# An eighth step of seven products in the second layer of an attention and gated-layer kernel, with a new order of all its steps

## The chip, the core and the metric

The kernel runs on one core of a Trainium2 chip. The metric is the device time of one execution in microseconds (us). Five engines work on it, each with a queue of its own that it takes strictly in order: TensorE (PE; its weight loads have a row of their own, PEld), VectorE (DVE), ScalarE (ACT), GpSimd (POOL) and SyncE (SP), which here issues almost all DMAs.

## What is computed

The reference is windowed attention with a few global keys, and a gated two-layer network on its result. Cut to what matters:

```python
# q, k, v: 4 batches, 8 heads, 768 positions, 64 per head; n_global = 8, n_local = 96
scores = matmul(q, k.T) / 8 + bias          # bias: -slope of the head * distance
keep = (pos_k < 8) | ((0 <= rel) & (rel < 96))
a = softmax(where(keep, scores, -1e9))
x = matmul(a, v)                            # 3072 tokens x 512
h = x @ w_in                                # 512 -> 2048
g = h * tanh(softplus(h))
out = g @ w_out                             # 2048 -> 512, float32
```

The two weights arrive as 64-bit floats and are turned into float32 on the chip. Products in full precision are made of three float16 products each: a number is split into a high half and a low rest, and high·high, high·low and low·high are summed.

## The kernel before

The 3072 tokens are cut into 12 chunks of 256 (two blocks of 128). Attention is done chunk by chunk in eight tiles t (a block and a pair of heads). The hidden layer is cut into eight steps of 256 hidden units. Step m = 8·chunk + fp stands for one step fp (0 to 7) of one chunk.

The order is written out by hand: `PROGRAM` (line 830) is a list of short commands, each a letter and a number. A loop at line 1036 calls the function of each, in a mode in which each engine gets its instructions in just that order. A mark ' behind a command gives its work to another engine. The commands that the prediction speaks of:

- `q`, `v`, `w`: loads of queries and keys, of values, of pieces of the weights. `A` to `E` turn a piece of the weights (0 to 31) into its halves.
- `s` (scores, PE), `t` (largest, DVE), `y` (exponentials, ACT), `g` and `p` (high half and rest of a tile, into a tile `hl` of a ring of three buffers), `X` (transposing DMA, frees the buffer), `W` (weighted sum of values, PE), `R`, `T`, `U`, `V` (rows of x, its halves, the transposing DMA). x's halves have a tile `xhl` of their own, in a ring of two.
- `i` (line 583): the first layer's product of a step, 24 matmuls of 256 columns into one of two `ph` banks. `j u n r` are four passes on ACT, `H` (line 607) the product that makes g and frees the bank.
- `z`, `Z`: high half and rest of g (tile `gt`). `o` (line 708) is the second layer's product of the step; it adds to the chunk's output in PSUM.
- `O` (line 397): a matmul of 512 columns on zeros, whose result nobody reads; there are 16.
- `k` (line 782): checks of ranges, whose last result `done_i` decides at the very end whether a slower program is to run.

A plain step `o` makes 12 matmuls of 512 columns: two token blocks, two hidden blocks, three half products (13 where one is cut in two). A fast step (`fast`, line 609) sees its two token blocks, two hidden blocks and two halves of the output's columns as a product of matrices of 2 by 2 blocks, and makes seven products of quarter blocks instead of eight: 7·3 matmuls of 256 columns. For that `J` (line 613) makes sums of g's blocks, so that `z` and `Z` work on 896 columns instead of 512, and `P`, `G`, `e`, `m` (lines 637 to 688) make, once for a step fp, the sums of w_out's quarters and their halves. Each of the seven products goes to one half of one of four PSUM banks: banks 0 and 1 are the output's, 2 and 3 hold what several quarters share. The corner `I` (line 732) reads banks 2 and 3 into a tile in SBUF, and the evacuation `Q` (line 743) adds that to banks 0 and 1. The list `FAST` (line 130) says from which chunk on a step fp is fast: 3 for fp 0 to 6, never for fp 7. So of each chunk from 3 on, seven steps are fast, and the eighth is plain: it writes banks 0 and 1 only, and banks 2 and 3 are through a step earlier.

```python
    FAST = (3,) * 7 + (NC,)
    PRODUCTS = ((0, 0, 2, 0), (2, 2, 0, 0), (6, 3, 0, 1), (1, 5, 1, 0), (3, 1, 3, 1), (5, 6, 2, 1), (4, 4, 3, 0))
```

An entry of `PRODUCTS` is the block of g, the block of weights, the bank and the half of the bank.

Of the kernel before, what the change touches and what calls it, by code (L numbers as in the profile page):

```python
# [108 lines left out]
def windowed(st, tc, loc):  # L109
# [20 lines left out]
    FAST = (3,) * 7 + (NC,)  # L130
# [642 lines left out]
    NX = 4 * NC  # L773
# [8 lines left out]
    def checks(i):  # L782
        if i == 0:
            nc.vector.tensor_scalar(ind[:, 0:2 * NC - 2], osum[:, 0:2 * NC - 2], 0.0, 0.0, op0=ALU.mult, op1=ALU.is_equal)
            nc.vector.tensor_scalar(ind[:, 2 * NC - 2:NX - 2], xmax, 1.0, None, op0=ALU.is_ge)
# [48 lines left out]
        s14 D1' S3' U1 y13 E1 O10 y12 g13' p10 W11 g12' t15 t14 A3' B3 C3 y14 S6' v2 D3' O12 A6 W10 p13 B6' C5 E2 s16 p12' t17 h2' y15 g14 w10 t16 p14 l2 y17 C6
        A10 y16 w8 w7 A8' O2 i0 B10 j0 g15' q5 g17 E3 D6' u0 p17' O13 s18 t18 x2 W13 S8 t19 W12 n0 w9 W14 p15 r0 y18 W15 w11 y19 D5 X17 E6 g16' O0 R2 V2 H0 B7
        s20 i1 g19 p16 z0' R3 t21 Z0 w12 T2 U2 p19 B8' y21 E5 X19 C8 V3 o0 t20 T3' U3 D8 j1 w14 S10' B9 u1 y20 A7 g21' i8 S7' h102 n1 C10 E8 C7 D7 s22 A9' p21'
        g20 l102 t23 j8 r1 X16 u8 H1 y23 p20 W17 X21 t22 n8 D10 B12 E7 X20 B11 w13 S11' z1' r8 i9 H8 w16 A12 g23' S12 Z1' W21 p23' y22 W16 A11 C12 E10 j9 A14'
        g22' g18 D12' X23 p22' u9 i2 C11 j2 n9 D11 X22 W19 p18' S14' r9 W20 S9' z8 B14' E11 u2 o1 H9 R4 C14 Z8 D14' E12' W23 i10 n2 r2 E14 X18 W22 w17 w18 T4 H2
        U4 w24 j10 u10 C9 W18 z2 n10 R5 z9 w20 D9' i3 Z2 Z9' o8 w15 r10 w19 w22 H10 j3 S18 A18' E9 S13' B16' q10 i11 S16' B18 A16 u3 S17' A17 C16 z10' A13' n3
        q7 C18 D16 B13' E16 o9 j11 C13 Z10' B17' C17 u11 D18 A20 E18' A15' r3 n11 D17 D13' E17 H3 E13' r11 B22' H11 w26 B20' S22' B15 A22' S24' v3 q6 z11 S20  # L840
        o10 i12 j12 z3' A19 u12 S15' C15 C22 i4 A24 D15' E15' w23 C20 Z3' w21 n12 B19' Z11' D20' B24 q8 r12 w25 S19 H12 o2 D22' A26 j4 u4 o3 C19 n4 E20 z12 C24
        r4 h3 D24 E22' D19' S21 B26 H4 N0 c7' E19 A21 S26' i5 j5 Z12' u5 S23' w27 B23 i13 B21' n5 C21 o11 A23 o12 C26 r5 E24' d7' D26 C23 H5 j13 A25 A27' z4'
        a7' u13 E26 V4 b7 S25' n13 B25' r13 i6 Z4' s24 H13 w29 C25 D21 D23 E23' z5 w28 t25 j6 i14 z13 u6 t24 n6 B27 S27' C27 q11 Z5' E21 T5 U5 D25 j14 w30 y24
        s26 r6 B28' D27 o4 A28 S28' g24' Z13' t26 o5 H6 c8 C28 p24 y26 w31 u14 E25 n14 V5 S30' z6' E27' t27 A30 D28' B30 o13 E28' C30 y27 l3 a8 r14 Z6 H14 D30
        A29' A31 S31 z14 y25 o6 E30 B31' g26 i7 d8' X24 i15 b8 p26' B29 Z14 C31 j7 g27 u7 n7 s28 r7 j15 u15 n15 v4 p27' S29' r15 q9 h4' H7 g25' a9 C29 o14 X27
# [197 lines left out]
```

## Time and profile before

| | before |
|---|---|
| median of 3 runs | 595.21 us (594.56 to 596.01) |
| the profiled execution | 594.36 us |
| its span, first to last instruction | 592.5 us |
| PE busy in the span | 577.9 us (98%) |
| DVE, ACT, POOL busy | 489.3, 478.3, 261.3 us |
| TensorE's granted clock | 1.0 of full speed |

The time of an execution is its span and 1.9 us around it. An engine's row on a page gives a group of instructions by line, tile and shape, their number, their busy time and the mean of one; behind the bar stands the idle time of the engine just before them, and what ended it. Matmuls overlap in the pipeline, so the busy time of one is more than the time by which it moves the next: for PE the prediction takes the distance between two starts.

### The profile page before, as it was taken

To read this page: it belongs to the slowest core of one execution; us is meant where nothing else is said; L and a number is where in the kernel's file an instruction comes from. 1 tells how busy PE (TensorE), PEld (TensorE's weight loads), DVE (VectorE), ACT (ScalarE), POOL (GpSimd) and SP (SyncE) were. 2 spreads that over 40 slices of the span, in tenths; PEclk is the share of its full clock that TensorE was granted. 3 is DMA by queue.
4 is the path that set the end of the run, shared out by engine and by line. 5 is a ranking of instruction groups with operands and counts; after the bars stand their busy time and mean duration, and the time that the engine had idled before them with its cause. 6 is when DMAs were issued, how large, how long until landed. Compare 5 with 4: busy or idle time off the path is not lost.

```text
span 592.5 us, 14936 instructions
## 1 busy us (share of the span) xinstructions
PE 577.9 (98%) x5652; PEld 466.6 (79%) x5652; DVE 489.3 (83%) x1272; ACT 478.3 (81%) x1112; POOL 261.3 (44%) x259
## 2 busy tenths in 40 slices
PE   6999999999999999999999999999999999999996
PEld 4887866567667789788889788888888888888884
DVE  6999999998999999989888986687888876663665
ACT  6999999999898998896786697677888678765661
POOL 0145422236316876552443474555563433444251
PEclk9999999999999999999999999999999999999999
DMA  9999999562562448654753653554574414240001
GB/s 228 312 276 191 254 308 242 151 148 66 118 150 55 114 95 137 100 117 122 166 115 68 126 127 80 94 118 107 88 178 58 101 38 90 54 91 19 36 2 38
DMA packets 132972, 73.76 MB, mean 124 GB/s; under 512 B 102144, under 2 KB 122624, under 8 KB 132896
## 3 DMA queue, kind: packets, MB, share of 16 engines
q1 hardware_dynamic: 132608, 72.63, 54.6%
q8 instruction: 45, 0.74, 0.5%
q14 instruction: 31, 0.25, 0.1%
q10 hardware_dynamic: 288, 0.14, 0.1%
HBM read 38.62 MB, written 6.29 MB: 76 GB/s over the span
## 4 chain that ended last, share of the span: by engine, by line
PE 77%; DVE 7%; DMA 6%; ACT 4%; issue 2%; POOL 2%; SPq 1%; DVEq 0%; POOLq 0%; ACTq 0%
PE ph L583 35%; PE pav L717 13%; PE po L717 10%; PE po L726 6%; PE sc L434 4%; PE sc L522 3%; PE pav L726 3%; DMA AT<-hl 2%; DMA vc<-v 2%; DMA wts<-w_in 1%; PE pav L518 1%; DMA qr<-qT 1%; DVE gf L607 1%; DVE gt L157 1%; DVE hl L157 1%
## 5 line engine op out<-in xcount | busy, mean ns | idle before, releaser
L583 PE MATMUL ph<-xT,wts 128*128 128x256 f16 x2304 | 265.6, 273 | 2.7 <-DVE gf L607 2.5
L583 PEld LDWEIGHTS <-wts 128*128 128x128 f16 x2304 | 222.3, 98 | 35.4 <-issue 5.4
L717 PEld LDWEIGHTS <-gt 128*128 128x128 f16 x1323 | 127.7, 98 | 16.7 <-issue 2.0
L157 POOL TENSOR_TENSOR gt<-gf,gt 128x896 f16<-128x896 f32 (+1 forms) x40 | 72.0, 1803 | 71.5 <-DVE gt L151 48.3
L590 ACT ACTIVATE e<-ph 128x512 f32<-128x512 f32 x96 | 56.4, 588 | 58.3 <-PE ph L583 55.9
L457 ACT ACTIVATE A<-A,nm 128x232 f32<-128x232 f32 (+1 forms) x192 | 88.3, 462 | 17.5 <-DVE nm L448 17.3
L607 DVE SCALAR_TENSOR_TENSOR gf<-e,ph 128x512 f32<-128x512 f32 x96 | 65.5, 682 | 32.1 <-ACT e L602 19.1
L157 POOL TENSOR_TENSOR hl<-A,hl 128x512 f16<-128x512 f32 (+1 forms) x39 | 47.5, 1224 | 78.5 <-DVE hl L151 48.4
L448 DVE CUSTOM_DVE_ANT_0 A<-sc,mb 128x232 f32<-128x232 f32 (+1 forms) x192 | 63.4, 375 | 11.7 <-PE sc L434 6.7
L726 PEld LDWEIGHTS <-gt 128*128 128x128 f16 x405 | 38.5, 98 | 40.8 <-issue 0.4
L598 ACT ACTIVATE e<-e,part 128x512 f32<-128x512 f32 x96 | 68.8, 717 | 2.1
L594 ACT ACTIVATE e<-e,ones 128x512 f32<-128x512 f32 x96 | 68.8, 717 | 1.8
L726 PE MATMUL po<-wts,gt 128*128 128x512 f16 (+1 forms) x309 | 68.4, 373 | 0.0
L157 DVE TENSOR_TENSOR gt<-gf,gt 128x896 f16<-128x896 f32 (+1 forms) x56 | 60.3, 1079 | 8.2 <-ACT gt L153 7.6
L157 POOL TENSOR_TENSOR wts<-ws,wts 128x512 f16<-128x512 f32 x22 | 30.0, 1366 | 74.0 <-ACT wts L153 28.0
L717 PE MATMUL pav<-wts,gt 128*128 128x256 f16 x378 | 62.0, 273 | 0.0
L602 ACT ACTIVATE e<-e 128x512 f32<-128x512 f32 x96 | 59.9, 624 | 1.7
L717 PE MATMUL po<-wts,gt 128*128 128x256 f16 x378 | 51.6, 273 | 0.0
L617 POOL TENSOR_TENSOR gf<-gf 128x128 f32<-128x128 f32 x41 | 23.2, 566 | 54.1 <-DVE gf L607 52.3
L151 DVE TENSOR_SCALAR gt<-gf 128x896 f16<-128x896 f32 (+1 forms) x51 | 31.5, 619 | 15.3 <-POOL gf L619 8.8
L153 ACT ACTIVATE gt<-gf 128x896 f16<-128x896 f32 (+1 forms) x45 | 36.5, 812 | 7.2 <-POOL gf L619 3.4
L457 ACT ACTIVATION_READ_ACCUMULATOR A<-A,nm 128x1 f32 x192 | 36.2, 189 | 0.0
(173 smaller groups left out, 900.8 us busy)
## 6 DMA issues: line engine op xcount, KB each, us to landing
qr<-qT SPq DMA_DIRECT2D x24, 256.0 KB
wts<-w_in SPq DMA_DIRECT2D x12, 512.0 KB
wts<-w_out SPq DMA_DIRECT2D x12, 512.0 KB
kr<-kd SPq DMA_DIRECT2D x32, 184.0 KB
out<-wr SPq DMA_DIRECT2D x11, 512.0 KB
vr<-v SPq DMA_DIRECT2D x10, 512.0 KB
vc<-vo SPq DMA_DIRECT2D x15, 192.0 KB
wr<-w_in SPq DMA_DIRECT2D x4, 512.0 KB
```

The source lines that it names most:

```text
L153: nc.scalar.activation(out, in_, AF.Copy, scale=scale)
L157: (nc.vector if other else nc.gpsimd).tensor_tensor(out, in_, high, op=ALU.subtract)
L448: nc.vector.tensor_tensor_reduce(out=A[:, j, 0:w], in0=sc[j][:, 0:w], in1=m, scale=-1.0 / (UNIT if ci < CF32 else UNIT * SQ), scalar=3.0e3 ...
L457: nc.scalar.activation(A[:, j], A[:, j], AF.Exp, bias=nm[:, h:h + 1], scale=-1.0, accum_out=rs[:, h:h + 1])
L583: nc.tensor.matmul(ph[:, j, :].rearrange("p (b t) -> p b t", b=2), wv4[:, 2 * fb, x, c * P:(c + 1) * P], xT[:, :, y * NCC + c, :], start=( ...
L590: nc.scalar.activation(mish[m]["e"], mish[m]["h"], AF.Exp, scale=1.0 / (SV * SW), accum_out=esum[:, m:m + 1])
L594: nc.scalar.activation(e, e, AF.Square, bias=ones)
L598: nc.scalar.activation(e, e, AF.Ln, bias=part, scale=SV * SW / SG / 2.0)
L602: nc.scalar.activation(e, e, AF.Exp, scale=-1.0)
L607: nc.vector.scalar_tensor_tensor(gf, mish[m]["e"], SG / (SV * SW), mish[m]["h"], op0=ALU.subtract, op1=ALU.mult, accum_out=gsum[:, m:m + 1])
L717: nc.tensor.matmul(pos[ci][bank][:, side * HN:(side + 1) * HN], gt[:, x, i, :], w[y], start=not begun[ci][bank], stop=n == 2 and fp == NFP ...
L726: nc.tensor.matmul(pos[ci][bank][:, c], gt[:, x, 2 * j + 1 - bank, :], wv4[:, 2 * fb + 1, y, c], start=not begun[ci][bank], stop=last and ...
```

## The change

`FAST` has 3 for all eight steps, and `fast` leaves out step 95, the last of the last chunk. So the eighth steps 31, 39, 47, 55, 63, 71, 79 and 87 become fast; step 95 stays plain. The weight sums of fp 7 have 4 KB per partition of their own (`four`), with all four quarter sums in one tile. The products stand in another order: the four for banks 2 and 3 first, the three for banks 0 and 1 last. In chunks 3 to 10 nothing is added to the second half of bank 1 any more; the corner writes that quarter of the output itself, with its sum for the checks (`osum3`), and `Q` adds one quarter less. x's halves have no ring of their own: they share the ring `hl` of three buffers. The whole table `PROGRAM` is replaced by another order, and several commands are given to another engine. The eight new steps bring eight commands `J` (31, 39, ..., 87) and `P7`, `G7`, `e7`, `m7`; the rest of the commands, the 16 `O` among them, are the same.

```diff
-    FAST = (3,) * 7 + (NC,)
+    FAST = (3,) * 8
...
+    four = cp.tile([P, 2, 4, DM // 2], F16, name="four")
...
+    osum3 = cp.tile([P, NC], F32, name="osum3")
+    nc.gpsimd.memset(osum3, 0.0)
...
-        xhl = at.tile([P, 2, DM], F16, name="xhl")
+        xhl = at.tile([P, 2, 2, W], F16, name="hl", bufs=3).rearrange("p a b w -> p a (b w)")
...
-        return ci >= FAST[fp]
+        return ci >= FAST[fp] and m != NC * NFP - 1
+
+    def whole_chunk(ci):
+        return all(fast(ci * NFP + fp) for fp in range(NFP))
...
+        elif fp == NFP - 1:
+            return (four,)
...
+        if fp == NFP - 1:
+            return [(w, four)]
...
+        if fp == NFP - 1 and k in (1, 4, 5, 6):
+            return [four[:, y, max(k - 3, 0), :] for y in range(2)]
...
-    PRODUCTS = ((0, 0, 2, 0), (2, 2, 0, 0), (6, 3, 0, 1), (1, 5, 1, 0), (3, 1, 3, 1), (5, 6, 2, 1), (4, 4, 3, 0))
+    PRODUCTS = ((0, 0, 2, 0), (5, 6, 2, 1), (3, 1, 3, 1), (4, 4, 3, 0), (2, 2, 0, 0), (6, 3, 0, 1), (1, 5, 1, 0))
...
-            for i, k, bank, side in PRODUCTS:
+            ends = {2: 1, 3: 3} if fp == NFP - 2 and not whole_chunk(ci) else {2: 1, 3: 3, 0: 5, 1: 6} if last else {}
+            for q, (i, k, bank, side) in enumerate(PRODUCTS):
...
+        if whole_chunk(ci):
+            into, total = out_tile(ci)[:, 0, HN:], osum3[:, ci:ci + 1]
+            nc.vector.scalar_tensor_tensor(into, end[:, 1, :], BACK, c[:, 1, :], op0=ALU.mult, op1=ALU.add, accum_out=total)
+            return
...
-        J91 r93 H93 j92 u92 z91' n92 i94 J93' r92 j94 u94 Z91' H92 J92' o90 z92' Z92 n94 z93' r94 H94 i95 J94 o91 j95 Z93' o92 o93 z94' u95 n95 Z94 r95 H95 k1
-        z95 Z95' k3 o94 I11 o95 Q11 k2
...
+        F0 j93 u93 n93 Y10 J89' z89' Z90 Z89 H91 i92 r93 J91 j92 H93 z91' u92 i94 J93 n92 Z91 j94 r92 H92 o89 J92' z92' u94 o90 z93' n94 Z92' r94 o91 i95 j95
+        o92 H94 u95 J94' Z93' n95 z94' k0 Z94 o93 r95 H95 z95' o94 Z95 I11' k1 o95 Q11 k3 k2
```

What the new order moves is shown at three places. The first is the end of DVE's queue (L739 to L741 are the corner, L753 the evacuation of the last chunk, L803 and L804 the last two of ten small operations of the third check, L809 and L810 the last check). Before:

```order
L803 TENSOR_SCALAR v_125<-v_125 1x1
L804 SCALAR_TENSOR_TENSOR v_125<-v_125,fl 1x1
L739 TENSOR_TENSOR vr<-vr 128x256
L740 SCALAR_TENSOR_TENSOR vr<-pav_8820,vr 128x512
L741 SCALAR_TENSOR_TENSOR vr<-pav_8820,vr 128x256
L753 SCALAR_TENSOR_TENSOR wr,osum<-po_8817,vr 128x512
L753 SCALAR_TENSOR_TENSOR wr,osum<-po_8818,vr 128x512
L809 TENSOR_SCALAR last<-sc 1x2
L810 SCALAR_TENSOR_TENSOR done_i<-last,v_125 1x1
L73 TENSOR_LOAD done_i
```

After, from the second evacuation on (L776); the next row is the one that writes `done_i`:

```order
L776 SCALAR_TENSOR_TENSOR wr,osum<-po_8916,vr 128x512
L819 TENSOR_SCALAR v_126<-sc 1x58
L820 TENSOR_REDUCE v_128<-v_126 1x1
L821 TENSOR_SCALAR v_128<-sc 1x1
L822 TENSOR_TENSOR v_128<-v_128 1x1
L823 TENSOR_REDUCE v_127<-sc 1x12
L824 TENSOR_REDUCE v_128<-v_127 1x1
L825 TENSOR_REDUCE v_128<-sc 1x1
L826 TENSOR_TENSOR v_128<-v_128 1x1
L827 TENSOR_SCALAR v_128<-v_128 1x1
L828 SCALAR_TENSOR_TENSOR v_128<-v_128,fl 1x1
L833 TENSOR_SCALAR last<-sc 1x2
```

The ten operations of the third check stood ahead of the corner, and stand between the last evacuation and the last check.

The second place is PE's queue at the same end; L794 and L818 are the third check's product. Before, between steps 93 and 94:

```order
L717 LDWEIGHTS gt
L717 MATMUL pav_8820<-qr,gt 128x256
L794 MATMUL sc<-ind,ones 1x145
L717 LDWEIGHTS gt
L717 MATMUL pav_8819<-wts,gt 128x256
```

After, behind the last product of step 95 (L739):

```order
L739 LDWEIGHTS gt
L739 MATMUL po_8916<-wts,gt 128x512
L818 MATMUL sc<-ind,ones 1x157
L831 MATMUL sc<-osum,ones 1x2
L73 TENSOR_LOAD done_i
```

The check's product went from ahead of step 94 to behind step 95.

The third place is the start of SP's queue, behind the first load of queries and keys (vo and vc are values, wts the weights, 512 KB a piece). Before; the next row is the second load of vo:

```order
L335 DMA wts<-w_in 128x4x256
L175 DMA qr<-qT 128x2x256
L178 DMA kr<-kd 64x2x264 x2
L215 DMA vo<-v 128x2x512
L232 DMA vc<-v 96x512
L233 DMA vc<-v 8x512
L175 DMA qr<-qT 128x2x256
L178 DMA kr<-kd 64x2x368 x2
L335 DMA wts<-w_in 128x4x256 x2
L337 DMA wts<-w_out 128x1024 x2
L175 DMA qr<-qT 128x2x256
L178 DMA kr<-kd 64x2x368 x2
```

After, the same stretch:

```order
L336 DMA wts<-w_in 128x4x256 x2
L176 DMA qr<-qT 128x2x256
L179 DMA kr<-kd 64x2x264 x2
L216 DMA vo<-v 128x2x512
L233 DMA vc<-v 96x512
L234 DMA vc<-v 8x512
L176 DMA qr<-qT 128x2x256
L179 DMA kr<-kd 64x2x368 x2
L338 DMA wts<-w_out 128x1024
L336 DMA wts<-w_in 128x4x256
L176 DMA qr<-qT 128x2x256
L179 DMA kr<-kd 64x2x368 x2
```

One piece of the weights moved ahead of the second load of queries and of the first values; ahead of the second chunk's values there are four pieces instead of five.

## Rows read from the trace of the kernel before

**Rows 1.** The page: the span, PE's busy time, the granted clock in 40 slices, and the chain that ended last by engine.

```profile
span 592.5 us, 14936 instructions
PE 577.9 (98%) x5652; PEld 466.6 (79%) x5652; DVE 489.3 (83%) x1272; ACT 478.3 (81%) x1112; POOL 261.3 (44%) x259
...
PEclk9999999999999999999999999999999999999999
...
PE 77%; DVE 7%; DMA 6%; ACT 4%; issue 2%; POOL 2%; SPq 1%; DVEq 0%; POOLq 0%; ACTq 0%
```

**Rows 2.** Busy time by stretch of the span: the stretch, its length, then busy us and number of instructions of PE, PEld, DVE, ACT and POOL, the granted clock, the DMA engines' busy share and GB/s.

```profile
0.00:60.00 60.00, 52.91 (x415) 41.93 (x416) 53.29 (x201) 52.27 (x155) 18.91 (x24) 1.00 1.00 251
60.00:150.00 90.00, 88.82 (x728) 61.60 (x726) 85.43 (x197) 87.72 (x192) 34.12 (x27) 1.00 0.75 195
150.00:200.00 50.00, 49.14 (x481) 33.61 (x479) 47.62 (x105) 46.21 (x107) 22.47 (x21) 1.00 0.52 107
200.00:260.00 60.00, 59.93 (x655) 50.62 (x654) 56.83 (x146) 54.23 (x134) 41.13 (x41) 1.00 0.59 114
260.00:560.00 300.00, 299.52 (x3148) 255.84 (x3145) 226.36 (x577) 224.89 (x506) 134.51 (x141) 1.00 0.45 93
```

**Rows 3.** PE in order of time in chunk 4, start and length in us: a fast step `o` from 281.48 until the `i` step at 283.77, and the plain eighth step from 286.39 until the attention's products at 288.98.

```profile
281.48 0.49 PE L717 MATMUL pav<-wts,gt 128*128 128x256 f16 x3
...
283.44 0.49 PE L717 MATMUL pav<-ws,gt 128*128 128x256 f16 x3
283.77 2.78 PE L583 MATMUL ph<-xT,wts 128*128 128x256 f16 x24
286.39 2.75 PE L726 MATMUL po<-wts,gt 128*128 128x512 f16 x13
288.98 0.25 PE L522 MATMUL sc<-vc,AT 104*128 104x64 f16 x3
```

**Rows 4.** The view of the waits: engine and line, what it waited for, us in total, how many waits, the longest.

```profile
ACT hl L153 <- DMA AT<-hl: 3.6, 3, 2.0
...
DVE hl L151 <- DMA AT<-hl: 3.0, 2, 2.4
...
PE ph L583 <- DVE gf L607: 2.5, 3, 1.2
...
PE sc L522 <- DMA AT<-hl: 0.8, 2, 0.4
```

**Rows 5.** Groups by line with different shapes apart: us busy, mean ns of one, idle time before them. The `gt` rows on DVE and POOL are `Z` with 896 and with 512 columns, the `hl` row is `p` on DVE.

```profile
L717 PEld LDWEIGHTS <-gt 128*128 128x128 f16 x1323 | 127.7, 98 | 16.7 <-issue 2.0 <-ACT A L457 0.2
...
L594 ACT ACTIVATE e<-e,ones 128x512 f32<-128x512 f32 x96 | 68.8, 717 | 1.8
...
L607 DVE SCALAR_TENSOR_TENSOR gf<-e,ph 128x512 f32<-128x512 f32 x96 | 65.5, 682 | 32.1 <-ACT e L602 19.1 <-POOL gt L157 8.9 <-POOL gf L619 1.8
L602 ACT ACTIVATE e<-e 128x512 f32<-128x512 f32 x96 | 59.9, 624 | 1.7
L590 ACT ACTIVATE e<-ph 128x512 f32<-128x512 f32 x96 | 56.4, 588 | 58.3 <-PE ph L583 55.9 <-DVE gf L607 1.9
...
L157 DVE TENSOR_TENSOR gt<-gf,gt 128x896 f16<-128x896 f32 x36 | 43.4, 1204 | 4.9 <-ACT gt L153 4.4
...
L157 DVE TENSOR_TENSOR hl<-A,hl 128x512 f16<-128x512 f32 x37 | 28.7, 776 | 1.5 <-ACT hl L153 1.5
...
L157 POOL TENSOR_TENSOR gt<-gf,gt 128x512 f16<-128x512 f32 x13 | 15.9, 1227 | 7.5 <-ACT gt L153 4.9 <-DVE gt L151 1.4 <-DVE rs L529 1.2
...
L641 DVE TENSOR_TENSOR vr<-wts 128x1024 f32<-128x1024 f16 x6 | 7.6, 1265 | 0.1
```

**Rows 6.** The start: PE in order of time, with the idle time before an instruction in brackets (28.18 is the first product with the second chunk's windows of values; 31.94 an `O`, 32.17 what follows it).

```profile
28.18 0.41 PE L518 MATMUL pav<-vc,AT 104*128 104x64 f32 x2 [0.73 <-DMA vc<-v]
...
31.94 0.39 PE L401 MATMUL po<-AT 128*128 128x512 bf16 x1
32.17 0.60 PE L480 MATMUL ph<-ident,A 128*128 128x128 f32 x4
```

**Rows 7.** The end in order of time: the third check's product and operations, the corner's first reading, the last step, the second evacuation, and the last check.

```profile
582.03 0.41 PE L794 MATMUL sc<-ind,ones 128*1 128x145 f32 x2
582.37 0.50 PE L717 MATMUL pav<-wts,gt 128*128 128x256 f16 x3
582.48 0.20 DVE L795 TENSOR_SCALAR v<-sc 1x46 f32<-1x46 f32 x1 [1.23 <-PE sc L794]
...
583.96 0.21 DVE L804 SCALAR_TENSOR_TENSOR v<-v,fl 1x1 f32<-1x1 f32 x1
...
584.55 0.60 ACT L153 ACTIVATE vr<-pav 128x512 f32<-128x512 f32 x1 [4.02 <-PE pav L717]
584.68 2.76 PE L726 MATMUL po<-wts,gt 128*128 128x512 f16 x13
...
587.47 0.69 DVE L753 SCALAR_TENSOR_TENSOR wr<-po,vr 128x512 f32<-128x512 f32 x1
...
588.22 0.19 PE L807 MATMUL sc<-osum,ones 128*1 128x2 f32 x2 [0.79 <-DVE wr L753]
588.45 0.15 DVE L809 TENSOR_SCALAR last<-sc 1x2 f32<-1x2 f32 x1 [0.28 <-PE sc L807]
588.63 0.21 DVE L810 SCALAR_TENSOR_TENSOR done_i<-last,v 1x1 int32<-1x1 f32 x1
```

More of the change, by code (lines that the diff above doesn't have):

```diff
@@ L713, in moe_out @@
         if fast(m):
-            for i, k, bank, side in PRODUCTS:
+            ends = {2: 1, 3: 3} if fp == NFP - 2 and not whole_chunk(ci) else {2: 1, 3: 3, 0: 5, 1: 6} if last else {}
+            for q, (i, k, bank, side) in enumerate(PRODUCTS):
                 w = factor(fp, k)
                 for n, (x, y) in enumerate(((0, 0), (0, 1), (1, 0))):
-                    nc.tensor.matmul(pos[ci][bank][:, side * HN:(side + 1) * HN], gt[:, x, i, :], w[y], start=not begun[ci][bank], stop=n == 2 and fp == NFP - 2 and (i, k) in ((5, 6), (4, 4)))
+                    nc.tensor.matmul(pos[ci][bank][:, side * HN:(side + 1) * HN], gt[:, x, i, :], w[y], start=not begun[ci][bank], stop=n == 2 and ends.get(bank) == q)
                     begun[ci][bank] = True
@@ L740, in corner, with out_tile @@
         nc.vector.scalar_tensor_tensor(c[:, 1:3, :], end, BACK, c[:, 3:4, :].broadcast_to([P, 2, HN]), op0=ALU.mult, op1=ALU.add)
+        if whole_chunk(ci):
+            into, total = out_tile(ci)[:, 0, HN:], osum3[:, ci:ci + 1]
+            nc.vector.scalar_tensor_tensor(into, end[:, 1, :], BACK, c[:, 1, :], op0=ALU.mult, op1=ALU.add, accum_out=total)
+            return
         nc.vector.scalar_tensor_tensor(c[:, 3, :], end[:, 1, :], BACK, c[:, 1, :], op0=ALU.mult, op1=ALU.add)
+    def out_tile(ci):
+        obs[ci] = raws.tile([P, DM, 2], I32, name="wr", bufs=3).bitcast(F32).rearrange("p f w -> p (f w)").rearrange("p (t m) -> p t m", t=2)
+        return obs[ci]
     def evacuate(ci):
         po = pos.pop(ci)
-        obs[ci] = raws.tile([P, DM, 2], I32, name="wr", bufs=3).bitcast(F32).rearrange("p f w -> p (f w)").rearrange("p (t m) -> p t m", t=2)
+        if ci not in obs:
+            out_tile(ci)
         for bank in range(2):
@@ L752, in evacuate @@
                 c = corners[ci]
-                nc.vector.scalar_tensor_tensor(obs[ci][:, t].rearrange("p (b m) -> p b m", b=2), po[bank].rearrange("p (b m) -> p b m", b=2), BACK, c[:, bank:bank + 3:2, :], op0=ALU.mult, op1=ALU.add, accum_out=osum[:, n:n + 1])
+                k = 1 if bank and whole_chunk(ci) else 2
+                nc.vector.scalar_tensor_tensor(obs[ci][:, t].rearrange("p (b m) -> p b m", b=2)[:, 0:k], po[bank].rearrange("p (b m) -> p b m", b=2)[:, 0:k], BACK, c[:, bank:bank + 2 * k - 1:2, :], op0=ALU.mult, op1=ALU.add, accum_out=osum[:, n:n + 1])
             if ci == NC - 1:
@@ L770, in flags @@
         nc.vector.tensor_scalar(fl[:, 3:4], L.n_f[0:1, 1:2], float(NLMAX), fl[:, 2:3], op0=ALU.is_le, op1=ALU.mult)
-    NX = 4 * NC
+    NX = 5 * NC
     NG = NC * NFP
@@ L834, in windowed @@
[L834 to L845, printed above, removed]
@@ new lines, in windowed @@
+        u74 i76 n74 T20' j76 U20 x11 u76 r74 X87 J72 n76 W83 H74 J74 W87 o70 X86 r76 W86 d23 z72' V20 o71 R21 s88 I8' t88 Z72 T21 y88 H76 t89 i75 U21 j75 J76
+        i77 g88' y89 u75 s90 Q8 z76' n75 j77 g89 o72 r75 t91 Z76 H75 o73 p89 u77 n77 p88' y91 z74 J75' t90 i78 V21 g91 z75 r77 s92 Z74 p91' j78 H77 X88 X89 Z75
+        u78 t92 Y8 t93 J77 y92 o74 n78 r78 y93 g92' i79 H78 g93' s94 j79 p92' u79 J78' y90 i80 t95 n79 X92 y95 z77' g90' p93 r79 j80 u80 o75 t94 z78 W89 Z77'
+        n80 X93 p90 H79 W92 o76 r80 J79' Z78 i81 y94 j81 z79' u81 H80 J80 n81 X91 o77 g95' r81 Z79' i83 o78 j83 p95' z80' g94 H81 i84 o79 p94' W88 W93 X94 u83
```

97 lines of the change are left out of this document (53 added, 44 removed).

## The prediction

> **What bounds the kernel now.** I read the page first: PE is busy 577.9 of 592.5 us, the clock is full throughout, and PE has 77% of the chain that ended last [rows 1]. The reader is to see that no other engine is above 83%. The table by stretch then says where there is room beside PE [rows 2]. From 260 to 560 us PE is busy 299.52 of 300 us while DVE and ACT have about 75 us to spare; there PE alone sets the pace. From 60 to 200 us all three are full: DVE is busy 133 of 140 us, ACT 134. So a product taken from PE is worth its whole length after 260 us, and ahead of that as long as DVE and ACT keep up. Last I read what PE waits for: apart from start and end little, 2.5 us for DVE's product that frees a bank of the first layer, 0.8 us for transposing DMAs [rows 4], and 0.73 us for the second chunk's windows of values [rows 6]. What PE does not do any more therefore comes off the end, if its waits stay as they are.
>
> **The eight eighth steps.** A fast step takes PE from 281.48 to 283.77, 2.29 us, the plain eighth step from 286.39 to 288.98, 2.59 us [rows 3]. That is 109 ns for a matmul of 256 columns and 216 for one of 512. The eight steps that become fast give 8 × (2.59 − 2.29) = **2.4 us**, all of it on PE. Each fast step has nine more matmuls, and so nine more weight loads of 98 ns [rows 5]. In the fast step shown, 21 of them hide behind the matmuls, so I take nothing for them; the bound on the other side is a rival below. The Trainium skill, page "TensorE: Matmul & The Clock Gate", section "Back-to-back issue gap", speaks against this edit: it gives a stream of loads and matmuls a spacing of 81 ns at 128 columns and 131 at 512. My estimate from it is 98 ns at 256, so a fast step would take 2.05 us and a plain one 1.57, and the eight steps would lose 3.8 us. The trace disagrees, with 109 and 216 ns in the rows named.
>
> **What the fast steps add beside PE.** `J` for eight steps, 896 instead of 512 columns in `z` and `Z`, and once `P7`, `G7`, `e7`, `m7`. At least six of the eight new steps lie after 260 us, where DVE has 74 us to spare [rows 2]; that work I cost at nothing. Step 31 and the weight sums lie between 150 and 260 us, and to be safe I count step 39 there too. On DVE they add 1.27 for `P7`, 1.38 for `m7` (the 1204 ns of 896 columns, scaled to 1024) and 2 × 0.5 for `Z`'s 384 more columns (the same row, scaled), some 3.7 us [rows 5], where DVE has 2.38 + 3.17 = 5.55 us idle [rows 2]. It fits; if it did not, each us over would be a us of PE. `Q` loses a quarter and the corner gains nothing, so nothing there.
>
> **The corner comes later.** Before, banks 2 and 3 were through a whole step ahead; now they are through only in the eighth step. The products' new order softens that: bank 2 is done after two of seven products, bank 3 after four. The tightest places are steps 47 and 87, behind which only one `i` step (2.62 us by the start of what follows [rows 3]) stands before the next chunk writes the banks. From bank 2's last product to there PE has 5 × 0.33 + 2.62 = 4.3 us, and the corner's reading and evacuation need 0.60 and four passes on DVE of at most 0.69 us [rows 7], 3.4 in all. The next chunk, moreover, begins with banks 2 and 3. I take nothing, with an upper bound of 8 × 0.3 us.
>
> **The end.** This is the part in which the new order costs. Before, the third check's product (0.34 us of PE, 582.03 to 582.37) and its ten operations on DVE (582.48 to 584.17, 1.69 us) run beside step 94. Then the second evacuation ends at 588.16, and the last check writes `done_i` at 588.84, 0.68 us later, after which only the fixed ending follows [rows 7]. Now the ten operations stand behind the second evacuation, DVE takes its queue in order, and `done_i` needs them: 1.69 + 0.39 for the last check and some 0.05 between, 2.13 us instead of 0.68. PE is spared the 0.34 us. The sum is 1.45 − 0.34 = **+1.1 us**. Nothing makes it smaller, since the ten follow the same evacuation in the same queue. It could be 0.35 more, since the second check's operations now stand between corner and evacuation. `done_i` is what the rows end with, so the output's store does not hide it. Step 95 itself moves closer to its `i`: three fast steps, 6.9 us, stand between them instead of four. Four passes on ACT (2.65 us), the product (0.68), a high half (at most as much) and a rest on POOL (1.23) make 5.3 us [rows 5]. That still fits.
>
> **The start.** Three `O` fewer stand behind the third `s` (seven instead of ten); they went to where PE waits for the first loads. An `O` moves what follows by 0.23 us (31.94 to 32.17 [rows 6]), so this gives between 0.7 us and nothing, if PE then waits instead; I take −0.3. One piece of the weights less is ahead of the second chunk's values. 512 KB at 251 GB/s [rows 2] are 2 us, more than the wait of 0.73 us [rows 6]. But another piece went ahead of the second queries and first values, which come 2 us later. The bounds are −0.73 and +2; I take −0.5, nearer the end at which a wait is seen.
>
> **All other moves.** The order of several hundred commands is new, and for the waits that come and go in the middle I have no term. The waits that are there, 2.5 + 0.8 us [rows 4], bound the gain; the loss is bounded by the rivals. I take nothing.
>
> **The sum.** −2.4 + 1.1 − 0.3 − 0.5 = −2.1 us. The profiled execution of 594.36 us would be 592.3; the median of 595.21 is 0.85 us above it, so the forecast is **593.1 us**.
>
> **Rivals.**
>
> - *The shared ring eats it.* A ring of three buffers that served 80 attention tiles serves 20 halves of x too. ACT and DVE wait 3.6 + 3.0 us on its transposing DMAs now [rows 4]. A quarter more users would add 1.7 us, and these waits fall where both engines are full. For it: the order that freed the tiles is another one. Against it: PE is behind them by a step or more in most places. Then 593.1 + 1.7 = 594.8 us, no difference that can be told (a measurement here tells 0.2%, some 1.2 us).
> - *DVE becomes the bound between 150 and 260 us.* The order gives DVE eight more of `p`, at up to 0.78 us [rows 5]. If all fell into that stretch, DVE would have 3.7 + 6.2 = 9.9 us more to do where it has 5.55 idle. It decides from 5.55 us on; at the full 9.9 PE waits 4.3 us more, and the time is 597.4 us: slower. Against it: they have 592 us to fall into.
> - *The new order waits less.* If it also removes the 3.3 us of waits in the middle, the time is 589.8, and half of them 591.5.
> - *Weight loads set the pace.* If the nine more loads of a fast step were exposed, 9 × 98 ns, an eighth step would take 0.58 us more than before, and the time would be 593.1 + 2.4 + 4.7 = 600.2 us. The fast steps of rows 3 speak against it. The page named above would have it go that way, with its smaller numbers.
>
> That the change does not do what it says I leave out: the eighth step's products on the new tile stand in PE's queue.
>
> **How the numbers follow.** The forecast has 0.48, with its own range of 592 to 594.2; the ring 0.25; DVE 0.13; fewer waits 0.13; weight loads 0.01. Faster by over 0.2% (below 594.0) are fewer waits and nearly all of the forecast, 0.13 + 0.44 = 0.57. Within it are the ring but for 0.01, and the forecast's upper edge, 0.28. Slower (above 596.4) are DVE, the weight loads and that 0.01, 0.15. For 8 in 10 I leave out weight loads, most of DVE's 597.4 and the far end of fewer waits: 590.8 to 596.6 us.
>
> **What the profile will show.** If I am right: 21 matmuls of 256 columns in 2.29 us for steps 31 to 87; in the last us ten small operations on DVE between the second evacuation and the last check, and `done_i` some 2.1 us behind the evacuation; no idle time of PE for the second chunk's windows; PE's waits in the middle between 2 and 5 us. PE idle before `i` with DVE as the cause between 150 and 260 us would show DVE as the bound. ACT or DVE idle before `hl` for transposing DMAs by much over 6.6 us would show the ring. If the first loads make PE wait for queries or values, my start is wrong.

## The result, and the profile after

The changed kernel takes 599.97 us (599.08 to 600.79, 6 runs) beside 595.19 us for the kernel before (594.53 to 596.36, 6 runs). The ratio is 1.0078, with a 95% interval of 1.0062 to 1.0093: it is slower by 4.6 us. Run again beside the later experiments it gave 599.75 us and 1.0065 (1.0051 to 1.0080). The prediction was 593.1 us, with a range up to 596.6: wrong in size and sign.

The profiled execution took 600.36 us, its span 598.6. First the page, as [rows 1]:

```profile
span 598.6 us, 15159 instructions
...
PE 578.9 (97%) x5713; PEld 473.4 (79%) x5716; DVE 503.6 (84%) x1293; ACT 482.2 (81%) x1119; POOL 273.6 (46%) x271
...
PEclk9998999999999999999999999999999999999999
...
PE 39%; DVE 5%; ACT 2%; issue 2%; POOL 1%; DMA 1%; DVEq 0%; POOLq 0%
```

The last row adds up to half the span only: the chain was followed back no further, and its shares are not to be set beside those of before. PE is no less busy than before, though it has less to do; the half clock of the fourth slice is a part of that. DVE is busy 14.3 us more, POOL 12.3. Busy time by stretch, with the columns of [rows 2]:

```profile
0.00:60.00 60.00, 52.48 (x385) 40.67 (x389) 50.90 (x190) 48.89 (x143) 17.36 (x25) 0.97 1.01 243
60.00:150.00 90.00, 90.00 (x756) 61.80 (x755) 85.17 (x215) 88.23 (x194) 32.89 (x26) 1.00 0.76 194
150.00:200.00 50.00, 49.14 (x478) 35.12 (x477) 47.49 (x104) 47.32 (x110) 24.19 (x22) 1.00 0.56 125
200.00:260.00 60.00, 58.84 (x633) 49.49 (x632) 55.99 (x134) 53.99 (x132) 43.94 (x44) 1.00 0.51 110
260.00:360.00 100.00, 96.47 (x1040) 82.89 (x1038) 86.67 (x212) 79.81 (x189) 50.12 (x53) 1.00 0.56 118
360.00:560.00 200.00, 198.87 (x2144) 175.49 (x2142) 153.99 (x382) 148.21 (x326) 90.00 (x90) 1.00 0.38 80
```

The same view of the kernel before, for the stretch in which PE lost most:

```profile
260.00:360.00 100.00, 99.98 (x1055) 85.07 (x1052) 87.22 (x216) 75.95 (x179) 42.33 (x43) 1.00 0.55 117
```

From 260 to 360 us PE, which was idle for 0.02 us, now stands still for 3.5 us. DVE is no busier there than before (86.67 against 87.22 of 100 us). So no engine is full, and still PE waits.

The waits, as [rows 4]:

```profile
DVE hl L152 <- DMA AT<-hl: 4.1, 4, 1.6
PE ph L586 <- DVE gf L610: 3.9, 5, 2.1
...
ACT hl L154 <- DMA xT<-hl: 1.7, 1, 1.7
```

PE's wait for `H` (now L610), which frees a bank of the first layer, grew from 2.5 to 3.9 us. The waits for `hl` fell from 6.6 to 5.8 us.

A fast eighth step (step 55) on PE in order of time, as [rows 3]:

```profile
383.27 0.49 PE L730 MATMUL pav<-wts,gt 128*128 128x256 f16 x3
383.60 1.15 PE L730 MATMUL pav<-four,gt 128*128 128x256 f16 x9
384.58 0.82 PE L730 MATMUL po<-wts,gt 128*128 128x256 f16 x6
385.23 0.49 PE L730 MATMUL po<-four,gt 128*128 128x256 f16 x3
385.56 1.69 PE L586 MATMUL ph<-xT,wts 128*128 128x256 f16 x14
```

It takes 2.29 us, as predicted.

PE's first large waits, with the idle time in brackets (50.88 transposes a block of x, 52.35 are scores, 54.41 is the first layer's step 8):

```profile
46.83 2.78 PE L586 MATMUL ph<-xT,wts 128*128 128x256 f16 x24
50.88 0.63 PE L565 MATMUL ph<-ident,x 128*128 128x128 f32 x4 [1.26 <-DVE xT L554]
52.35 1.73 PE L437 MATMUL sc<-kr,qr 64*128 64x232 f32 x8 [0.84 <-DVE nm L451]
54.01 0.61 PE L404 MATMUL po<-AT 128*128 128x512 bf16 x1
54.41 3.88 PE L586 MATMUL ph<-xT,wts 128*128 128x256 f16 x24
```

The same place by stretch, with the columns of [rows 2]:

```profile
51.00:53.00 2.00, 1.16 (x9) 0.90 (x10) 2.00 (x6) 0.99 (x2) 0.71 (x2) 1.00 0.88 188
53.00:55.00 2.00, 2.00 (x11) 1.02 (x8) 1.97 (x5) 2.00 (x8) 0.87 (x1) 0.56 1.29 205
55.00:57.00 2.00, 2.00 (x13) 1.48 (x11) 2.00 (x4) 2.00 (x4) 0.00 (x0) 0.59 1.44 119
```

Two waits for DVE come one after the other, and behind them the granted clock falls from 1.0 (2.4 GHz) to 0.5 (1.2 GHz): 24 matmuls last 3.88 us instead of 2.78.

The largest wait in the middle, on PE, then on DVE, then on POOL (302.48 is `Z43`, 304.60 `p60`, 306.58 `H44`; on POOL 301.84 is `Z42`, 303.75 `d17`, the rest of some keys):

```profile
304.76 0.49 PE L730 MATMUL po<-wr,gt 128*128 128x256 f16 x3
307.32 2.79 PE L586 MATMUL ph<-xT,wts 128*128 128x256 f16 x24 [2.07 <-DVE gf L610]
```

```profile
302.48 2.19 DVE L158 TENSOR_TENSOR gt<-gf,gt 128x896 f16<-128x896 f32 x1
304.60 2.06 DVE L158 TENSOR_TENSOR hl<-A,hl 128x512 f16<-128x512 f32 x1
306.58 0.67 DVE L610 SCALAR_TENSOR_TENSOR gf<-e,ph 128x512 f32<-128x512 f32 x1
```

```profile
301.84 1.89 POOL L158 TENSOR_TENSOR gt<-gf,gt 128x896 f16<-128x896 f32 x1 [1.10 <-DVE gt L152]
303.75 2.36 POOL L158 TENSOR_TENSOR wc<-kr,wc 128x736 f16<-128x736 f32 x1
```

PE waits for `H44`, and `H44` waits for nothing but its turn on DVE. The two operations ahead of it take twice and three times what such operations take alone (1.08 and 0.68 us). Each began while POOL was at work, and each ended its own length less 0.14 us after POOL's instruction. Such an operation is called held below: it begins while an instruction of POOL runs, and lasts over 0.15 us longer than the median of the same operation on the same shape when none does.

The start and the end, as [rows 6, 7] (35.16 waits for keys; at the end the second evacuation and `done_i`):

```profile
15.07 0.66 PE L521 MATMUL pav<-vo,AT 128*128 128x64 f32 x4 [0.52 <-DMA vo<-v]
...
35.16 1.68 PE L437 MATMUL sc<-kr,qr 64*128 64x232 f32 x8 [0.16 <-DMA kr<-kd]
37.26 2.78 PE L586 MATMUL ph<-xT,wts 128*128 128x256 f16 x24
...
592.57 0.69 DVE L776 SCALAR_TENSOR_TENSOR wr<-po,vr 128x512 f32<-128x512 f32 x1 [0.58 <-PE po L739]
...
594.99 0.21 DVE L834 SCALAR_TENSOR_TENSOR done_i<-last,v 1x1 int32<-1x1 f32 x1
```

### The profile page after: what moved, and what is told of

Read it like the earlier page. It is cut to its first block, busy times and chain, and to the rows that moved or that the text cites. A ratio compares the mean times of both kernels' runs of the same rounds, so it can differ in the third digit from the quotient of the medians.

```text
span 598.6 us, 15159 instructions
## 1 busy us (share of the span) xinstructions
PE 578.9 (97%) x5713; PEld 473.4 (79%) x5716; DVE 503.6 (84%) x1293; ACT 482.2 (81%) x1119; POOL 273.6 (46%) x271
## 4 chain that ended last, share of the span: by engine, by line
PE 39%; DVE 5%; ACT 2%; issue 2%; POOL 1%; DMA 1%; DVEq 0%; POOLq 0%
PE ph L586 19%; PE pav L730 10%; PE po L730 7%; PE sc L437 2%; PE sc L525 1%; DVE gt L158 1%; DVE gf L610 1%; DMA AT<-hl 1%; DVE hl L557 1%; DVE gf L624 1%; ACT A L460 0%; ACT e L601 0%; DVE hl L158 0%; PE po L739 0%; DVE gt L152 0%
## 5 line engine op out<-in xcount | busy, mean ns | idle before, releaser
L730 PEld LDWEIGHTS <-gt 128*128 128x128 f16 x1491 | 143.1, 98 | 21.5 <-issue 2.5
L158 POOL TENSOR_TENSOR gt<-gf,gt 128x896 f16<-128x896 f32 (+1 forms) x42 | 75.8, 1808 | 63.3 <-DVE gt L152 38.8
L610 DVE SCALAR_TENSOR_TENSOR gf<-e,ph 128x512 f32<-128x512 f32 x96 | 65.5, 682 | 30.1 <-ACT e L605 21.6
L730 PE MATMUL pav<-wts,gt 128*128 128x256 f16 x402 | 66.3, 273 | 1.3 <-POOL gt L158 0.8
L158 POOL TENSOR_TENSOR hl<-A,hl 128x512 f16<-128x512 f32 (+1 forms) x31 | 36.6, 1182 | 55.5 <-DVE hl L152 30.5
L158 POOL TENSOR_TENSOR wts<-ws,wts 128x512 f16<-128x512 f32 x21 | 27.2, 1298 | 68.8 <-ACT wts L154 21.4
L623 POOL TENSOR_TENSOR gf<-gf 128x128 f32<-128x128 f32 x43 | 27.5, 640 | 68.0 <-DVE gf L610 66.8
L730 PE MATMUL po<-wts,gt 128*128 128x256 f16 x426 | 58.1, 273 | 0.0
L739 PEld LDWEIGHTS <-gt 128*128 128x128 f16 x301 | 28.7, 98 | 31.6 <-issue 0.6
L152 DVE TENSOR_SCALAR gt<-gf 128x896 f16<-128x896 f32 (+1 forms) x50 | 34.3, 688 | 16.5 <-POOL gf L625 13.1
L158 DVE TENSOR_TENSOR hl<-A,hl 128x512 f16<-128x512 f32 (+1 forms) x49 | 43.8, 898 | 4.5 <-ACT hl L154 4.2
L739 PE MATMUL po<-wts,gt 128*128 128x512 f16 x205 | 46.7, 378 | 0.0
```

The source lines that it names most:

```text
L158: (nc.vector if other else nc.gpsimd).tensor_tensor(out, in_, high, op=ALU.subtract)
L610: nc.vector.scalar_tensor_tensor(gf, mish[m]["e"], SG / (SV * SW), mish[m]["h"], op0=ALU.subtract, op1=ALU.mult, accum_out=gsum[:, m:m + 1])
L739: nc.tensor.matmul(pos[ci][bank][:, c], gt[:, x, 2 * j + 1 - bank, :], wv4[:, 2 * fb + 1, y, c], start=not begun[ci][bank], stop=last and ...
```

## The experiments

Times are given by the ratio to the kernel before, applied to its 595.2 us.

### The order without the fast eighth steps, and the fast eighth steps without the order

The new order with plain eighth steps:

```diff
-    FAST = (3,) * 8
+    FAST = (3,) * 7 + (NC,)
-    ... J31 ... J39 ... J47 ... J55 ... J63 ... J71 ... J79 ... J87 ... P7 ... G7 ... e7 ... m7
```

> The new order and the shared ring, but with the eighth steps plain as before (no J for them, no P7, G7, e7, m7). Theory A, the new order's own waits cost the time, and the fast eighth steps give their 2.4 us in any order: 600.0 + 2.4 = 602.4 us (601 to 603), with PE's waits near 49, 305 and 477 us still there. Rival B, what the fast eighth steps add on DVE, ACT and GpSimd makes the waits: below 597 us, and those waits are gone.

Measured: ratio 1.0034 (1.0020 to 1.0048), 597.2 us, +2.0. Neither theory had all of it, though the interval reaches below B's 597 us. The waits at 49 and 305 us are there, as A said (305 is 1.49 us instead of 2.23 by the starts), those at 343, 346 and 477 are gone, as B said. So the order, with its shared ring, costs 2 us, and the fast eighth steps, which spare PE 2.4, cost 2.6 more. These are times of all runs; the traced execution of this run took 599.59 us, its longest, so that its trace ends only 0.8 us ahead of the changed kernel's.

The old order with fast eighth steps, put in by hand:

```diff
-        xhl = at.tile([P, 2, 2, W], F16, name="hl", bufs=3)
+        xhl = at.tile([P, 2, DM], F16, name="xhl", bufs=1)
...
 PROGRAM of the kernel before:
-    H31 ... I3 ... o31
+    H31 J31' ... o31 I3
```

> The order of the kernel before with the eight eighth steps made fast (their J behind H on GpSimd, P7, G7, e7 and m7 behind m6, each corner behind its eighth step); x's halves keep a tile of their own, one instead of two, since three shared ones can't serve that order. Theory A: 595.2 - 2.4 = 592.8 us (592.2 to 594.0), no new waits of PE above 1 us. Rival B: the added work makes waits in any order: 596 to 600 us.

Measured: 1.0554 (1.0525 to 1.0582), 628.2 us. A fell, and B's size was far too small. PE waits for `H` 13.3 us (2.5 before) and for transposing DMAs 10.0 us (0.8 before). Part of this may be the one tile for x instead of two, the few `T` and `V` that moved with it, and the corners that stand later on DVE; the run doesn't say how much. It shows that the fast eighth steps do not simply fit into that order, and it left the added work to be tried by itself.

### The added work alone, in the old order

Plain products, but `J`, `z` and `Z` as a fast eighth step needs them:

```diff
-        return slice(1, 8) if fast(m) else slice(0, 4)
+        return slice(1, 8) if fast(m) else slice(0, 7) if 31 <= m < 95 and m % NFP == 7 else slice(0, 4)
...
 PROGRAM of the kernel before:
-    H31
+    H31 J31'
...
```

> The kernel before, unchanged in order and with plain eighth steps on TensorE, but J stands behind H for the eight eighth steps 31 to 87 (on GpSimd) and their z and Z work on 896 instead of 512 columns, as fast eighth steps would need; the sums of fp 7's weights are not made. Theory A, the added work fits beside PE: within 1 us of the kernel before, 594.5 to 596.2 us. Rival B, it makes PE wait for DVE and GpSimd: 598 to 602 us, with DVE's operations held more often behind GpSimd's.

Measured: 1.0129 (1.0088 to 1.0170), 602.9 us, +7.7. B is right, its range a little low for the point. This run takes nothing from PE and moves nothing else. DVE is 10.4 us busier in it (499.7 us against 489.3), POOL 21.3 (282.6 against 261.3), and DVE's 103 us of idle time did not hide that. 101 operations of DVE are held, for 53.2 us together, instead of 83 for 46.3. PE's rows show where it came out (transposes behind `p`, `Z61` on POOL, an `H`):

```profile
335.40 0.26 PE L522 MATMUL sc<-vc,AT 104*128 104x64 f16 x3 [0.99 <-DMA AT<-hl]
...
337.17 0.26 PE L522 MATMUL sc<-vc,AT 104*128 104x64 f16 x3 [0.88 <-DMA AT<-hl]
...
415.33 0.28 PE L717 MATMUL pav<-wts,gt 128*128 128x256 f16 x1 [1.57 <-POOL gt L157]
...
448.49 1.69 PE L583 MATMUL ph<-xT,wts 128*128 128x256 f16 x14 [1.21 <-DVE gf L607]
```

Three kinds of result come late, none by more than 1.6 us, at the ends of chunks 5 and 7 and in chunk 8. On POOL `Z61` stands right behind `J63`. Two runs split the added work. Only the eight `J`, on POOL, with nothing waiting for their sums:

> The kernel before with the eight J of steps 31 to 87 on GpSimd and nothing else: z and Z keep 512 columns, so no later operation waits for these sums. Theory G, what cost 7.7 us together is the longer way of an eighth step from H over J, z and Z to its product at the chunk's end: the sums alone cost under 2 us, below 597 us. Rival H, it is the load on GpSimd and the operations of DVE held behind it: 599 to 602 us.

Measured: 1.0055 (1.0036 to 1.0074), 598.5 us, +3.3, between the two theories. The eight `J`, of 1.9 to 2.9 us each on POOL, make an engine that is busy 44% busier by 17.3 us, and they alone cost 3.3 us; DVE operations are held behind POOL 96 times instead of 83. The wait for `Z61` behind `J63` is here too, though nothing waits for the sums of `J63`:

```profile
414.44 0.28 PE L717 MATMUL pav<-wts,gt 128*128 128x256 f16 x1 [1.58 <-POOL gt L157]
```

Of the other three waits one for a transpose is left, of 0.85 us. The rest of the 7.7 us comes with the wider `z` and `Z`. The added work again, with these `J` on DVE:

> As the run with the added work in the old order (J and 896 columns in z and Z for steps 31 to 87, plain products), but these eight J on DVE. Their way is 1.0 us long there instead of some 1.7 to 2.4 on GpSimd. Theory G (the way of the eighth step is what costs): 598 to 600 us instead of 602.4. Rival F (what stands ahead of the next H on DVE is what costs): 602 to 606 us.

Measured: 1.0088 (1.0053 to 1.0123), 600.4 us, +5.2. The point lies nearer G, but the interval meets that of the run before; it does not tell G from F. The same move in the changed kernel (`J31'` and five more without their mark; two stood on DVE already):

> The changed kernel with the J of the eighth steps on DVE (seven of eight move from GpSimd). Theory G: the waits at 342 and 346 us shrink and the time is 598 to 599.5 us. Rival F: more stands ahead of later H on DVE, 601 to 603 us.

Measured: 1.0088 (1.0054 to 1.0122), 600.4 us: nothing that can be told from the changed kernel. The waits at 342 and 346 us stand (0.38 and 0.83 us idle), so G's first sentence fell here.

### What stands ahead of H on DVE

All `J` from step 31 on moved from POOL to DVE:

```diff
-    J31' J33 J34' ...
+    J31 J33 J34 ...
```

> The changed kernel with J of the steps from 31 on all on DVE (37 move from GpSimd). DVE gets 37 x 1.0 = 37 us more, GpSimd loses some 63. Theory E, what costs is DVE held behind GpSimd and the sums' way over two engines: the held time falls from 56 to some 40 us, H comes no later, and the time is 597 to 598.5 us. Rival F, H is late because too much stands ahead of it on DVE: each J puts 1.0 us ahead of a later H, PE waits more, 602 to 608 us.

Measured: 1.0265 (1.0239 to 1.0292), 611.0 us. F is right and even too low. The held time did fall, from 56.2 to 49.2 us, but PE waits 11.6 us for `H` instead of 3.9, and that is 7.7 of the 11.2 us by which this run is slower than the changed kernel. So most of what these operations cost on DVE is the delay of the next `H` behind them.

One collision taken away, `d17` on POOL moved behind `J45`:

```diff
-    g61' s62 d17 q17 ... J45'
+    g61' s62 q17 ... J45' d17
```

> The changed kernel with GpSimd's d17 moved behind J45, so that nothing runs on GpSimd beside DVE's p60 at 304.6 us. Theory E, a DVE operation on SBUF that begins while GpSimd works waits for the end of GpSimd's instruction: p60 takes 0.7 us instead of 2.06, H44 comes 1.4 us earlier, and PE waits 0.9 us there instead of 2.23. Rival: p60 is long for a reason of its own; it stays at 2 us and so does the wait.

Measured at the place, on DVE (`p60` and `H44`), then on PE:

```profile
304.75 0.68 DVE L158 TENSOR_TENSOR hl<-A,hl 128x512 f16<-128x512 f32 x1
305.35 0.68 DVE L610 SCALAR_TENSOR_TENSOR gf<-e,ph 128x512 f32<-128x512 f32 x1
```

```profile
306.09 2.79 PE L586 MATMUL ph<-xT,wts 128*128 128x256 f16 x24 [0.70 <-DVE gf L610]
```

`p60` takes 0.68 us instead of 2.06, and PE's wait is 0.87 us by the starts instead of 2.23: E, to the tenth, at this one place. The one execution took 599.54 us.

### The clock, and waits taken away

Ten matmuls on zeros in the waits at 49 and 51 us:

```diff
-    V3 ... s22
+    O16 O17 O18 O19 O20 O21 V3 ... O22 O23 O24 O25 s22
```

> The changed kernel with ten more matmuls on zeros, six where PE waits at 49.5 us and four where it waits at 51.3 us. Theory C, TensorE's clock fell to half at 53.2 us because PE stood idle there: the granted clock stays 1.0, the first layer's step at 54.4 us takes 2.6 us again instead of 3.8, and the time is 1.1 to 1.3 us less, 598.8 us; the two waits for DVE themselves stay, filled. Rival: the fall is not due to the idle time: it stays, and the time stays at 600.0 us.

The clock stayed at 1.0 there, and step 8 took its 2.79 us again:

```profile
54.38 2.79 PE L586 MATMUL ph<-xT,wts 128*128 128x256 f16 x24
```

So C's mechanism is right: steps from there to 305 us start 1.1 us earlier than in the changed kernel. The gain did not last. By 343 us 0.5 us of it was left, and the ratio is 1.0081 (1.0053 to 1.0109), 600.0 us: C's time fell. Five places reordered at once:

```diff
-    T2' z0' g19' R3 ... t21 ... U2 ... C8 V3 ... t20 T3' ... U3 ... s22
+    T2' g19' R3 U2 ... t21 ... V3 ... t20 ... T3' U3 ... s22 z0' C8
-    p60' o41 H44
+    o41 H44 p60'
-    p69' U15 z48' ... H50 ... J50' I5 Z48        J74 W87 ... R21
+    p69' z48' ... Z49 Z48 j51 H50 U15 ... J50'   W87 ... W86 R21 J74
-    H95 z95' o94 Z95 I11' k1 o95 Q11 k3 k2
+    H95 k1 z95' k3 o94 Z95 I11' o95 Q11 k2
```

> The changed kernel with five places reordered: at the start R3, U2, t21, t20, T3 and U3 ahead of other work on DVE; H44 ahead of p60; U15 behind H50 and Z48 ahead of J50; R21 ahead of J74; and the third check ahead of step 94 as before. Theory A: the waits there go, 600.0 - (3.4 + 2.0 + 1.4 + 1.3 + 1.3) = 590.6 us (590 to 593). Rival D, the waits are only passed on, since DVE and ACT are late at the next place too: 595 to 599 us.

Measured: 1.0091 (1.0064 to 1.0117), 600.6 us. D is right in kind; the time lies above its range. The waits at 305 and 477 us are gone, and step 8 came 2.5 us earlier, at 51.91; then PE waited where it had not before, for a half of values and, at 316.85, for `H` again:

```profile
51.91 2.79 PE L586 MATMUL ph<-xT,wts 128*128 128x256 f16 x24 [0.28 <-DVE xT L554]
57.17 0.22 PE L525 MATMUL pav<-vc,AT 104*128 104x64 f16 x2 [2.44 <-DVE vc L249]
...
316.85 4.20 PE L586 MATMUL ph<-xT,wts 128*128 128x256 f16 x24 [2.02 <-DVE gf L610]
```

The last row's 4.20 us are the clock again, at 0.5 from 318 us on. The fall of the clock alone does not make the changed kernel slow, though: three of the six runs of this version had a mean clock of 0.999 or 1.0, and they took 599.1 to 601.4 us. Last, a version meant to win: fast eighth steps only in chunks 8 to 10, and the third check put back:

```diff
-    FAST = (3,) * 8
+    FAST = (3,) * 7 + (8,)
```

> The changed kernel with eighth steps fast only in chunks 8 to 10 (71, 79, 87) and plain in chunks 3 to 7, and with the third check ahead of step 94 as before. Theory A with the end as measured: 597.1 for the order with plain eighths, less 0.6 for the end and 3 x 0.3 for the three steps, whose added work lies where DVE has room: 595.6 us (595.0 to 596.4). Rival: late eighth steps cost as much as early ones: 597.5 us or more.

Measured: 1.0033 (1.0015 to 1.0051), 597.2 us, between the two: the three late steps and the end together gained nothing over the order alone. The wait of 1.3 us for `R21` near 477 us, which the order alone does not have, came back with step 71. With that wait and the clock mended too:

> The run with late fast eighth steps (71, 79, 87) and the third check ahead of step 94, and with two mends more: ten matmuls on zeros in the waits at 49 and 51 us, so that the clock stays up, and R21 ahead of J74 on DVE, so that TensorE does not wait for it near 477 us. Theory A, waits removed where H has room stay removed: 597.2 - 1.1 - 1.3 = 594.8 us (594.3 to 596.0). Rival D, they are passed on as in the run with all five places: 596.5 to 598 us.

Measured: 1.0053 (1.0035 to 1.0071), 598.4 us: D. In the trace the clock was full, the wait at 477 us was gone, and a new one of 1.3 us stood at 502 us. No version beat the kernel before. The control:

> The changed kernel itself, beside the others on this chip: 599 to 601 us by its earlier runs. If it is 602 us or more, or spread over 2 us, runs of kernels with little room ahead of TensorE differ more from one to the next than those of the kernel before, and differences of 1 us between the experiments tell nothing.

Measured: 599.75 us (599.03 to 600.34), 1.0065 (1.0051 to 1.0080). Differences under some 1.5 us between experiments are not told apart here.

### The end alone

The kernel before with the second and third check at the end, as in the changed kernel:

```diff
-    H95 k1 z95 Z95' k3 o94 I11 o95 Q11 k2
+    H95 z95 Z95' o94 I11 k1 o95 Q11 k3 k2
```

> The kernel before with one move only: the second and third check stand at the end as in the changed kernel (the second behind the last corner, the third behind the last evacuation). Theory A, the term of the end is right: 595.2 + 1.45 - 0.34 = 596.3 us (595.9 to 596.6), and done_i comes 1.9 to 2.1 us behind the evacuation instead of 0.68. Rival: the output's store ends later than the checks, and nothing changes: 595.2 us.

Measured: 1.0008 (0.9996 to 1.0020), +0.5 us. From the end of the second evacuation to that of `done_i` it is 1.92 us, in the changed kernel 1.94, before 0.68. The delay is as A said. The time does not decide: its interval, from −0.2 to +1.2 us, takes in nothing as well as A's 1.1.

## Why the prediction was wrong

**Eight eighth steps, −2.4: right.** Seven of them take 2.29 us, or 2.39 where scores follow, against 2.59 and 2.69 in the order with plain ones; step 47 takes 2.86 us, by a wait for `H` behind it. The nine more weight loads cost nothing, so the rival of the weight loads fell, though its 600.2 us came close to the time.

**Added work beside PE, 0: the step that failed.** Of the steps after 260 us, "where DVE has 74 us to spare", it said: "that work I cost at nothing". That took idle time for room. In the old order this work, without the weight sums of fp 7, cost 7.7 us. In the new one it cost 5.0: 2.6 between the order alone and the changed kernel, and the 2.4 that PE was spared. The two have the same order of steps, and between their traces the loss lies where the prediction put nothing: the changed kernel starts step 40 at 270.5 us, 0.6 us ahead of the order alone, and step 55 at 360.2 us, 1.9 us behind it. So the weight sums and step 31, ahead of 260 us, are not where it was lost. From 260 to 360 us PE is idle 3.5 us in the changed kernel and 1.6 with the order alone:

```profile
260.00:360.00 100.00, 98.36 (x1041) 83.39 (x1040) 82.17 (x208) 81.22 (x190) 47.27 (x50) 1.00 0.56 117
```

Most of the 13 us in which DVE is idle there lie between operations that wait for PE, ACT or POOL, and at 302 us two operations of 1.08 and 0.68 us ahead of an `H` that was due took 2.19 and 2.06 beside POOL. The room that counts is the time from the end of `H` to the `i` step that needs its bank. Taken from the traces for the 16 or 17 `i` steps of that stretch, its median is 2.1 us before, 1.5 with the order alone and 0.4 after; before, none of these steps had under 0.6 us, with the order alone six have it, after eight. From the last pass on ACT to the start of `H` it is 1.2 us on average before, 1.8 in the order alone, 2.4 after, mostly DVE's queue. The order took a part of the room, and the added work the rest.

**All other moves, 0: failed too, by less.** Order and ring alone cost 2.0 us, where the prediction's end and start make +0.3. In the trace of the order alone stand the two waits for DVE at 49 and 51 us, with the half clock behind them, and the one for `H` at 305 us, of 1.33 us; that they make up the 2.0 us is not shown. PE's waits from 60 to 560 us, which the prediction put at 2 to 5 us, are 6.7 us by the rows of busy time, where they were 2.6.

**The end, +1.1: right in mechanism.** `done_i` ends 1.94 us behind its evacuation, not 2.13, since neighbouring operations overlap a little. What it costs in time is not told: alone in the old order +0.5 us, with an interval from −0.2 to +1.2.

**The start, −0.8: it did not come.** The wait of 0.73 us for the second chunk's windows is gone. But the piece of weights moved ahead brought a part of the other bound: 0.52 us for the first values, 0.16 for keys. The first `i` step starts at 37.26 us, and at 36.80 in the second trace of the changed kernel; in the trace of before it is 37.00.

**Corner later, 0: right.** No wait of PE for a bank of the output shows.

**The rivals.** The shared ring did not cost in waits (5.8 us against 6.6), but no run takes it out of the order. "DVE becomes the bound between 150 and 260 us" had the right engine and a time 2.4 us short, but not the place or the form: PE is 1.1 us less busy there (its sign, waits of 0.39 and 0.69 us for `H`, did show) and 3.5 us less from 260 to 360, and DVE is not full. What was missing among the rivals is that an engine with idle time can be late everywhere.

Still open is how the 5 us of added work divide between DVE's queue, POOL's load and the longer way of the step; the runs show a price for `J` on POOL (3.3 us for eight in the old order) and for `J` on DVE (11.2 us for 37 in the new one), neither of them all of it, and none tells the longer way apart. Why single mends do not add up is shown in part: gains made before 305 us are lost to the next `H` or to the clock. Why the last version, whose profiled execution starts the product of step 92 at 581.0 us where the one before it has 582.0, and took 597.92 us against 598.98, shows nothing of that in its ratio over all runs is not settled.

## What to carry to other kernels

Idle time of an engine in a stretch is not room for more work. Before work is added beside a bound engine, read from the trace how early each result that it waits for is there, count what stands ahead of that result in its engine's queue, and take the added work's full length, held time included, for the bound of its price wherever that margin is smaller. An order that was fitted to one set of operations has its margins there; a few more operations per step, even off the path, can need the whole order fitted again, and here the new order alone cost nearly as much as the steps spare.

## What the runs showed of the hardware

**DVE held behind POOL.** In the changed kernel 99 operations of DVE are held, for 56.2 us together; before it was 83 and 46.3 us. The difference is 9.9 of the 14.3 us that DVE is busier. But for three of them a held operation ends its own length less 0.14 us after POOL's instruction, whatever its size: even one on 128x8 elements goes from 0.16 to 0.92 us (at 198.4 us). None of them reads PSUM: 46 of the 96 `H`, which do, begin beside POOL, and none takes more than 0.69 us. The run without the neighbour at 304.6 us (2.06 us to 0.68) shows it on a single operation. The Trainium skill, page "SBUF — State Buffer", section "Who interferes with whom", says that a DVE instruction with two SBUF inputs contends with a GpSimd instruction that reads SBUF, since its second input comes through the port that the two share, and that one with at most one SBUF input, outside the two-port modes, does not. The trace agrees for `p60`, which reads two tiles in SBUF, and for `H`, which reads one in SBUF and one in PSUM.

**The clock fell behind waits, and not always behind the same one.** In the first profile of the changed kernel it fell at 53.2 us for 3.4 us; in the second, with the same waits, it stayed up there and fell behind the wait at 303 us:

```profile
303.00:305.00 2.00, 0.51 (x5) 0.21 (x3) 2.00 (x2) 1.94 (x5) 1.37 (x1) 1.00 0.00 0
...
307.00:309.00 2.00, 2.00 (x11) 1.44 (x10) 1.68 (x4) 0.00 (x0) 0.80 (x2) 0.50 0.91 219
```

Step 46 then starts 1.7 us earlier than in the first, and step 49 only 0.1 us: the one fall cost about what the other did. All ten runs of the changed kernel have a mean clock of 0.995 or 0.996. Of 21 runs of the kernel before beside four of the experiments, 14 have 0.998 or more and take 594.3 to 596.6 us, five have 0.996 or less and take 596.4 to 599.2.
